# Loads of q and k on ScalarE's queue, and six conversions instead of eight in the first stage behind a rotary attention

## The chip, the cores and the metric

The kernel runs on one core of a Trainium2 chip. The metric is the device time of one execution in microseconds. The engines are TensorE (PE, matmuls), VectorE (DVE), ScalarE (ACT), GpSimd (POOL) and SyncE (SP), which only issues DMA transfers. Each works through its own instructions in the order in which the program has them; they wait for each other with semaphores, and the transfers that they issue run beside them.

## The reference

```python
q_rot, k_rot = (rotate(q), rotate(k))              # q, k, v: (4, 8, 576, 64), rotary positions
scores = scale * np.matmul(q_rot, k_rot.transpose(0, 1, 3, 2))
attn = softmax(scores)                              # over the last axis
x = np.matmul(attn, v)                              # then (2304 tokens, 512)
...
h = x @ w_in                                        # 512 -> 2048
g = np.where(h >= 1, h, np.where(h <= -1, 0.0, (h + 1) ** 2 / 4))
x = g @ w_out                                       # 2048 -> 512
...
h = x @ w_in2
r = np.maximum(h, 0.0)
out = (s * (r * r) + b) @ w_out2
```

## The kernel before

**Numbers.** Every product is made of three matmuls on two halves (hi and lo) of each operand, so all operands are split: hi by a copy on ACT, lo by a subtraction on POOL or DVE. The weights of the two MLPs arrive as 64-bit words and are *converted* to such halves, 512 columns at a time (`Slice.convert`, L126): ACT L133, DVE L134 to L137, ACT L138, and four pieces on POOL (L96). A conversion needs a raw tile (`wraw`, two buffers, load at L144) and two scratch tiles (`wa`, `wm`) from one of two pools with one buffer each, chosen by the half of the slice. A weight slice is one sixteenth of the hidden units of a layer, and has two halves. Some halves are converted early and *parked* in device memory (`parkd`), from where they are later only loaded (`w<-parkd`, L153).

**Attention.** The heads go in 16 pairs, each with 9 units of 128 rows, so 144 units. For a unit: scores on PE (`sc`, L352, two buffers), row maxima on DVE (`nm`, L354), exponentials on ACT (`p`, L359), transposes and the product with v on PE. For pair i, while pair i-1 is being computed, `rope_pair` rotates q and k (POOL and DVE); `lay_q` writes q's halves to `qs` (ACT L306, DVE L307, the last readers of the q tile), and `lay_k` leaves k's halves in the loaded tile, from where SP copies them to `kh` (L323, four transfers) and `kz` (L324, two). The tiles of q and k are loaded by `load_qk` (L261, 576 KB each) two pairs ahead, for pair i+2 at units 4 (q) and 6 (k) of pair i (`do_load`). There are four buffers (`QB`), so q of pair i+2 takes the memory of q of pair i and has to wait until `qs` of pair i is written; k of pair i+2 waits until the copies `kh<-kin` and `kz<-kin` of pair i have landed. From unit 48 on, work of the first MLP on finished tokens is run between the units (`beside`, results added up in device memory as `yd`, tiles `ys` and `yq`, L498 to L506); conversions and parking also lie there.

**Stages.** Behind the attention `stage` (L694) does the rest of the first MLP in three calls: a (the last tokens, 3 chunks of 288, with the first half of the hidden units, `set_a`), b (4 chunks, the second half, `set_b`) and c (2 more). A stage is a loop over chunks and slices; step (c, f) makes the hidden units f of chunk c (`hps`, then ACT L201 and L202, DVE L204, ACT `gh` L102, DVE `gl` L106), and the second layer (`yps`, L764 to L766) follows three steps (`GL`) later. The slices that the next stage needs stand in the list `pending`, one entry for each half. At each step that counts (not step 0 of the first chunk and not the first three of a later one) `owed` grows by `per`, and for each whole one `convert_next` converts the next entry; parked entries at the head of the list are loaded at once by `load_next`.

**Order.** The order of the instructions on PE behind the attention is that of the code; on the other engines, and within the attention, a scheduler sets it when the kernel is built, from priorities and from `issue_after` marks, and it lays each DMA on the queue of the engine that the code names.

Of the kernel before, what the change touches and what calls it, by code (L numbers as in the profile page):

```python
# [66 lines left out]
def kernel(ctx, tc, qq, kk, vv, tab, ww1, ww2, s, b, out):  # L67
    nc = tc.nc
    dram = ctx.enter_context(tc.tile_pool(name="dram", bufs=1, space=DRAM))
    xd = dram.tile([KD, P, NT], F32, name="xd")  # L70
    xp = dram.tile([2, KD, P, NT], F32, name="xp")
    yd = dram.tile([GA // G1, KD, P, NT], F32, name="yd")
    zd = dram.tile([KD, P, NT], F32, name="zd")
    y1d = dram.tile([KD, P, NT], F32, name="y1d")
# [150 lines left out]
    set_a = [Slice(wpa, ww1, f, ROOMS[f]) for f in range(GA)]  # L225
    scratch = [wst]
    set_b = [Slice(None, ww1, f, ROOMS[f - GA], parkd) for f in range(GA, NF)]
# [29 lines left out]
    def load_qk(i, nm, pieces=WHOLE):  # L257
        bb, hp = divmod(i, NP)
        t = att2.tile([P, 2, S], F32, tag="qkin", name=f"{nm}in", bufs=QB)
        for c in pieces:  # L260
            nc.sync.dma_start(out=t[:, :, c], in_=(qq if nm == "q" else kk)[bb, hp, :, :, c])  # L261
        qk_in[nm, i] = t

    def load_v(i):
# [188 lines left out]
    def load_parts(x, n0, n):  # L453

        for t in range(2):
            nc.sync.dma_start(out=x[t].bitcast(F32), in_=parts_at(t, n0, n))
        return x
# [53 lines left out]
    for c in HALVES:  # L511
        nc.sync.dma_start(out=tab_sb[:, :, c], in_=tab[:, :, c])
        if c is HALVES[0]:
            load_qk(0, "k", HALVES)
    load_qk(0, "q", HALVES)
    tq, tk = qk_in.pop(("q", 0)), qk_in.pop(("k", 0))

# [14 lines left out]
    with tc.issue_after(first):  # L532
        load_qk(1, "k")
        load_qk(1, "q")
        load_v(0)
        nc.sync.dma_start(out=s_sb, in_=s.to_broadcast([P, 1]))
        nc.sync.dma_start(out=b_sb, in_=b.to_broadcast([P, 1]))
# [115 lines left out]
    set_c = [Slice(wpa, ww2, f, ROOMS[f]) for f in range(GA)]  # L653
# [40 lines left out]
    def parts_tiles(n):  # L694
        return [qx.tile([P, KD, n], F32R, tag=t, name=t + "2") for t in ("xh", "xl")]
# [316 lines left out]
    def cut(n0, n1, n):  # L1012

        k = -(-(n1 - n0) // n)
        at = [n0 + (n1 - n0) // 16 * i // k * 16 for i in range(k + 1)]
        return [(a, b - a) for a, b in zip(at, at[1:])]
# [5 lines left out]
    a, b, c, d = cut(last, NT, N2A), cut(0, last, N2), cut(last, NT, N2), cut(0, NT, N2)  # L1022
# [45 lines left out]
    def mix(one, two):  # L1068

        both = []  # L1070
        for i, sl in enumerate(one):
            both += [sl] + two[i * len(two) // len(one):(i + 1) * len(two) // len(one)]
        return both

    twice = lambda sls: [sl for sl in sls for _ in range(2)]
    left = twice(set_d[:4] + set_d[7:])
# [22 lines left out]
    first_b, first_c1 = [], []  # L1099

    def ahead_of(chunk, tiles):
        tiles.extend(parts_tiles(chunk[1]))
        load_parts(tiles, *chunk)

    stage(xd, a, yd[0], None, set_a, act1, twice(set_b), 0.5, after=lambda: ahead_of(b[0], first_b))
    assert not pending
    stage(None, b, y1d, yd[1], set_b, act1, mix(left, twice(set_c)), 0.85, ready=first_b, after=lambda: ahead_of(c[0], first_c1))
    stage(None, c, y1d, yd[0], set_b, act1, [], 0.9, lambda i, mark: front_c(i + GA - 1, mark), ready=first_c1)
    convert_next()
    assert not pending and not raws2 and not stores  # L1110
# [66 lines left out]
```

## Time and profile before

| | us |
|---|---|
| three runs, median (lowest to highest) | 1131.36 (1127.6 to 1132.65) |
| profiled execution, its own time | 1134.72 |
| its span, first to last instruction | 1132.9 |
| busy: PE / DVE / ACT / POOL | 1082.3 / 776.5 / 630.0 / 424.7 |
| mean granted TensorE clock | 0.989 |

In the profiled execution the attention without MLP work between the units runs to about 145 us, with it to about 446, stage a to about 548, stage b to about 668 and stage c to about 720; then the second MLP follows. "SPq" in a row is SP's sequencer issuing a transfer. A row of the waits says which line on which engine waited for which, how long in total, how many times, and the longest.

### The profile page before, as it was taken

Reading aid. Unit: us, or ns where it says so; the run is one execution under the profiler, and the core shown is the slowest. Engines: PE = TensorE matmul, PEld = TensorE weight load, DVE = VectorE, ACT = ScalarE, POOL = GpSimd, SP = SyncE. Lnnn points to the kernel's source line nnn. Section 1 sums busy time; section 2 is a strip of 40 time slices with the busy share of each in tenths; the row PEclk is TensorE's granted clock in tenths of the full one; section 3 lists DMA queues with packets and bytes.
Section 4 is the critical chain, followed back from the end, with each engine's and each line's share of the span. In section 5 each row is a group of like instructions: output and inputs, shape, how many; then the busy total and the mean of one; then the engine's idle time right before and its main releaser. Section 6 shows DMA issues by size and latency. Waiting matters only on the chain.

```text
span 1132.9 us, 20034 instructions
## 1 busy us (share of the span) xinstructions
PE 1082.3 (96%) x7296; PEld 990.5 (87%) x7296; DVE 776.5 (69%) x1449; ACT 630.0 (56%) x1430; POOL 424.7 (37%) x564
## 2 busy tenths in 40 slices
PE   3998898989999999999999999999999999999998
PEld 3666687778988989989999999999999999999997
DVE  6888887776676663365566656975877767667754
ACT  4777776765667765455454545475445438334421
POOL 7869886975453241343344444500211110000000
PEclk9999898999999999999999999999999999999999
DMA  7565855665667652854567662521242753221210
GB/s 224 164 174 170 236 154 177 206 174 177 197 190 216 175 173 85 269 171 130 179 203 239 211 230 89 161 68 46 73 143 90 263 172 107 81 64 59 80 61 35
DMA packets 109762, 173.24 MB, mean 153 GB/s; under 512 B 29408, under 2 KB 80608, under 8 KB 109664
## 3 DMA queue, kind: packets, MB, share of 16 engines
q1 hardware_dynamic: 109664, 171.97, 48.5%
q8 instruction: 57, 0.93, 0.4%
q14 instruction: 41, 0.34, 0.1%
HBM read 110.10 MB, written 48.56 MB: 140 GB/s over the span
## 4 chain that ended last, share of the span: by engine, by line
PE 71%; DVE 8%; DMA 8%; POOL 5%; issue 3%; ACT 3%; SPq 1%; POOLq 0%; DVEq 0%; ACTq 0%
PE sum L914 13%; PE hps L180 12%; PE yps L830 6%; PE yps L828 6%; PE yps L829 6%; PE sc L352 5%; PE h L180 3%; PE av L400 3%; PE tp L374 3%; PE y L180 3%; PE yps L765 3%; PE yps L766 3%; PE yps L764 3%; DMA yd<-yq 2%; POOL kin L96 2%
## 5 line engine op out<-in xcount | busy, mean ns | idle before, releaser
L180 PE MATMUL hps<-xh,w 128*128 128x288 f32 (+4 forms) x640 | 164.0, 325 | 0.0
L354 DVE TENSOR_REDUCE nm<-sc 128x1 f32<-128x576 f32 x144 | 107.9, 751 | 43.5 <-PE sc L352 42.6
L352 PE MATMUL sc<-kh,qs 128*128 128x288 f32 x336 | 105.5, 335 | 28.4 <-ACT p L359 16.7
L359 ACT ACTIVATE p<-sc,nm 128x576 f32<-128x576 f32 x144 | 106.7, 744 | 33.5 <-DVE nm L354 32.7
L922 ACT ACTIVATE four<-four,b_sb,s_sb 128x480 f32<-128x480 f32 x64 | 47.3, 782 | 138.1 <-DVE four L921 138.1
L830 PE MATMUL yps<-gh,w 128*128 128x480 f32 (+1 forms) x320 | 118.6, 370 | 0.0
L828 PE MATMUL yps<-gh,w 128*128 128x480 f32 (+1 forms) x320 | 118.4, 370 | 0.0
L829 PE MATMUL yps<-gl,w 128*128 128x480 f32 (+1 forms) x320 | 118.4, 370 | 0.0
L180 PEld LDWEIGHTS hps<-xh,w 128*128 128x128 f32 x640 | 113.7, 189 | 1.0
L96 POOL TENSOR_TENSOR wm<-wm,w 128x256 f32<-128x256 f32 x80 | 70.6, 903 | 105.2 <-ACT w L138 63.6
L352 PEld LDWEIGHTS sc<-kh,qs 128*128 128x128 f32 x336 | 65.8, 198 | 47.7 <-ACT p L359 25.8
L180 PE MATMUL hps<-xl,w 128*128 128x288 f32 (+4 forms) x320 | 103.8, 324 | 0.0
L352 PE MATMUL sc<-kz,qs 128*128 128x288 f32 x336 | 96.5, 306 | 0.0
L764 PE MATMUL yps<-gh,w 128*128 128x288 f32 (+3 forms) x288 | 93.5, 325 | 2.5 <-ACT gh L102 1.9
L374 PE MATMUL tp<-ident,p 128*128 128x128 f32 x576 | 90.8, 283 | 5.1 <-ACT p L359 3.3
L765 PE MATMUL yps<-gl,w 128*128 128x288 f32 (+3 forms) x288 | 93.6, 325 | 0.7 <-DVE gl L106 0.7
L766 PE MATMUL yps<-gh,w 128*128 128x288 f32 (+3 forms) x288 | 93.4, 324 | 0.0
L374 PEld LDWEIGHTS tp<-ident,p 128*128 128x128 f32 x576 | 73.1, 145 | 8.1 <-ACT p L359 3.7
L180 PE MATMUL y<-gh,w 128*128 128x288 f32 x320 | 74.8, 305 | 3.5 <-ACT pt L377 1.7
L180 PE MATMUL h<-xh,w 128*128 128x288 f32 x320 | 74.0, 308 | 2.9 <-DVE gl L106 2.9
L400 PE MATMUL av<-pt,vin 128*64 128x256 f32 (+1 forms) x512 | 76.1, 422 | 0.2
L106 DVE TENSOR_TENSOR gl<-hps,gh 128x288 fp32r<-128x288 f32 (+4 forms) x88 | 46.2, 526 | 34.1 <-ACT gh L102 34.1
(154 smaller groups left out, 2846.1 us busy)
## 6 DMA issues: line engine op xcount, KB each, us to landing
wraw<-in_ww SPq DMA_DIRECT2D x58, 512.0 KB, 4.5
w<-parkd SPq DMA_DIRECT2D x24, 512.0 KB, 6.6
parkd<-wraw SPq DMA_DIRECT2D x18, 512.0 KB, 3.0
kin<-in_k SPq DMA_DIRECT2D x15, 576.0 KB, 5.0
qin<-in_q SPq DMA_DIRECT2D x15, 576.0 KB, 4.2
kh<-kin SPq DMA_DIRECT2D x60, 144.0 KB, 2.6
xs<-y1d SPq DMA_DIRECT2D x32, 240.0 KB, 2.6
xd<-u SPq DMA_DIRECT2D x16, 288.0 KB, 2.5
```

The source lines that it names most:

```text
L180: m = nc.tensor.matmul(out_ps, l, r, start=(i == 0), stop=(i == n - 1))
L352: nc.tensor.matmul(sc[:, half, o:o + n], l, r[:, k0:k0 + n], start=m == 0, stop=m == len(todo) - 1)
L354: maxs[i * 9 + k] = nc.vector.tensor_reduce(out=nm, in_=sc[:, :, :288], axis=AX.XY, op=ALU.max, negate=True).ins
L374: m = nc.tensor.transpose(v[:, c, :], p[:, c * P:(c + 1) * P], ident)
L400: nc.tensor.matmul(ps[j * D:(j + 1) * D, :n], v[:, kt, j, :], pt[g][:, kt, j, :], start=kt == 0, stop=False)
L764: nc.tensor.matmul(acc, wh, gh, start=f == 0, stop=False)
L765: nc.tensor.matmul(acc, wh, gl, start=False, stop=False)
L766: nc.tensor.matmul(acc, wl, gh, start=False, stop=last)
L828: nc.tensor.matmul(acc, wh, gh, start=f == 0, stop=False)
L829: nc.tensor.matmul(acc, wh, gl, start=False, stop=False)
L830: nc.tensor.matmul(acc, wl, gh, start=False, stop=last)
L914: nc.tensor.matmul(acc, l, r, start=j == 0, stop=j == len(t) - 1)
```

## The change

Two things. In `load_qk` the loads of q and k for pairs 2 to 15 (14 + 14 transfers) are issued by ACT instead of SP. And the first stage converts or loads ahead for six slices of `set_b` instead of all eight (12 entries, of which 6 are parked, instead of 16 with 8 parked), at 0.36 for each counting step instead of 0.5, so 6 conversions instead of 8; the second stage begins with the two slices left over (two loads of parked halves, two conversions) and has 0.88 for each step instead of 0.85, which is 19 conversions instead of 18, and the third stage does 9 instead of 8. The total is unchanged.

```diff
@@ load_qk
-            nc.sync.dma_start(out=t[:, :, c], in_=(qq if nm == "q" else kk)[bb, hp, :, :, c])
+            (nc.scalar if i > 1 else nc.sync).dma_start(out=t[:, :, c], in_=(qq if nm == "q" else kk)[bb, hp, :, :, c])
@@ the calls of stage
-    stage(xd, a, yd[0], None, set_a, act1, twice(set_b), 0.5, after=lambda: ahead_of(b[0], first_b))
+    stage(xd, a, yd[0], None, set_a, act1, twice(set_b[:6]), 0.36, after=lambda: ahead_of(b[0], first_b))
     assert not pending
-    stage(None, b, y1d, yd[1], set_b, act1, mix(left, twice(set_c)), 0.85, ready=first_b, after=lambda: ahead_of(c[0], first_c1))
+    stage(None, b, y1d, yd[1], set_b, act1, twice(set_b[6:]) + mix(left, twice(set_c)), 0.88, ready=first_b, after=lambda: ahead_of(c[0], first_c1))
     stage(None, c, y1d, yd[0], set_b, act1, [], 0.9, lambda i, mark: front_c(i + GA - 1, mark), ready=first_c1)
```

The scheduler then puts the instructions of the attention into another order in places. Where the load of q and k for pair 12 stands shows what moves. On SP before, `kin_2705` is k of pair 10, whose memory `kin_3526` (k of pair 12) takes; `qin_3439` is q of pair 12:

```order
L144 DMA wraw_3248<-in_ww1 128x512
L451 DMA xp_58<-xl_2739 128x4x288
L466 DMA xs_3115<-xd_57 128x288
L324 DMA kz0_109<-kin_2705 64x576
L323 DMA kh_2887<-kin_2705 64x576 x4
L324 DMA kz0_109<-kin_2705 64x576
L261 DMA qin_3439<-in_q 128x1152
L144 DMA wraw_3441<-in_ww1 128x512
L261 DMA kin_3526<-in_k 128x1152
L268 DMA vin_2936<-in_v 128x5x64
```

On ACT now, at the same units (`qs0` is pair 10's, `qin_2642` its q tile, whose memory `qin_3439` takes):

```order
L306 ACTIVATE qs0_107<-qin_2642 64x576
L133 ACTIVATE wa_3044<-wraw_3042 128x512
L359 ACTIVATE p_2763,sums_2438<-sc_2773,nm_2778 128x576
L261 DMA qin_3439<-in_q 128x1152
L414 ACTIVATE sume_2867<-sums_2438,eps_67 128x4
L138 CAST w_2357<-wm_3045 128x512
L433 COPY r_2805<-rm_2800 128x384
L379 COPY pt_2765<-tp_2829 128x4x128
L359 ACTIVATE p_2818,sums_2810<-sc_2811,nm_2816 128x576
L261 DMA kin_3526<-in_k 128x1152
L359 ACTIVATE p_2818,sums_2810<-sc_2835,nm_2840 128x576
```

The two loads have left SP, where raw weights and v now follow the copies of pair 10 directly; on ACT the q load stands behind an exponential, and the k load between two exponentials.

On SP at the start of stage a, before (`yd<-yq` are the last stores of `beside`, `wraw_6264` a raw load for the stage's conversions):

```order
L717 DMA xs2_6458<-xd_57 128x288
L451 DMA xp_58<-xl2_6058 128x4x288
L144 DMA wraw_6264<-in_ww1 128x512
L506 DMA yd_59<-yq_5882 128x288
L506 DMA yd_59<-yq_5901 128x288
L498 DMA yq_5920<-yd_59 128x288
L498 DMA yq_5939<-yd_59 128x288
L153 DMA w_6031<-parkd_62 128x2x512 x2
L506 DMA yd_59<-yq_5920 128x288
L153 DMA w_6560<-parkd_62 128x2x512 x2
L506 DMA yd_59<-yq_5939 128x288
L153 DMA w_6261<-parkd_62 128x2x512 x2
```

And now:

```order
L717 DMA xs2_6443<-xd_57 128x288
L451 DMA xp_58<-xl2_6058 128x4x288
L506 DMA yd_59<-yq_5882 128x288
L506 DMA yd_59<-yq_5901 128x288
L498 DMA yq_5920<-yd_59 128x288
L498 DMA yq_5939<-yd_59 128x288
L153 DMA w_6031<-parkd_62 128x2x512 x2
L506 DMA yd_59<-yq_5920 128x288
L153 DMA w_6659<-parkd_62 128x2x512 x2
L506 DMA yd_59<-yq_5939 128x288
L153 DMA w_6327<-parkd_62 128x2x512 x2
L144 DMA wraw_6330<-in_ww1 128x512
```

The raw load has gone from ahead of the stores to behind them and the parked weights; the parked loads still stand among the stores.

On DVE in stage a before, from the eighth block of hidden units (`hps_6281`) on; L134 to L137 with `wa_6267` are one conversion, those with `wa_6478` the next:

```order
L204 SCALAR_TENSOR_TENSOR hps_6281<-hps_6281,ac_6294 128x288
L134 TENSOR_SCALAR wm_6268<-wa_6267 128x512
L106 TENSOR_TENSOR gl_6299<-hps_6281,gh_6298 128x288
L135 SCALAR_TENSOR_TENSOR wm_6268<-wa_6267,wm_6268 128x512
L136 TENSOR_SCALAR wa_6267<-wm_6268 128x512
L134 TENSOR_SCALAR wm_6479<-wa_6478 128x512
L204 SCALAR_TENSOR_TENSOR hps_6314<-hps_6314,ac_6327 128x288
L137 SCALAR_TENSOR_TENSOR wa_6267<-wraw_6264,wa_6267 128x512
L135 SCALAR_TENSOR_TENSOR wm_6479<-wa_6478,wm_6479 128x512
L106 TENSOR_TENSOR gl_6332<-hps_6314,gh_6331 128x288
L136 TENSOR_SCALAR wa_6478<-wm_6479 128x512
L137 SCALAR_TENSOR_TENSOR wa_6478<-wraw_6279,wa_6478 128x512
```

And now, from just ahead of the same block:

```order
L134 TENSOR_SCALAR wm_6250<-wa_6249 128x512
L135 SCALAR_TENSOR_TENSOR wm_6250<-wa_6249,wm_6250 128x512
L136 TENSOR_SCALAR wa_6249<-wm_6250 128x512
L137 SCALAR_TENSOR_TENSOR wa_6249<-wraw_6144,wa_6249 128x512
L204 SCALAR_TENSOR_TENSOR hps_6261<-hps_6261,ac_6274 128x288
L106 TENSOR_TENSOR gl_6279<-hps_6261,gh_6278 128x288
L204 SCALAR_TENSOR_TENSOR hps_6294<-hps_6294,ac_6307 128x288
L134 TENSOR_SCALAR wm_6502<-wa_6501 128x512
L106 TENSOR_TENSOR gl_6312<-hps_6294,gh_6311 128x288
L135 SCALAR_TENSOR_TENSOR wm_6502<-wa_6501,wm_6502 128x512
L136 TENSOR_SCALAR wa_6501<-wm_6502 128x512
L137 SCALAR_TENSOR_TENSOR wa_6501<-wraw_6330,wa_6501 128x512
```

The conversions follow one another where two had been interleaved, with three instructions of the stage between them.

## Rows read from the trace of the kernel before

**Rows 1.** By stretch: busy PE, PEld, DVE, ACT, POOL; PE's clock, DMA share, GB/s.

```profile
25.00:145.00 120.00, 110.02 (x768) 80.21 (x767) 100.04 (x167) 86.45 (x202) 100.40 (x133) 0.97 0.66 188
145.00:446.00 301.00, 284.59 (x2169) 251.22 (x2169) 209.58 (x377) 201.27 (x494) 164.19 (x226) 0.98 0.58 173
446.00:550.00 104.00, 100.83 (x736) 99.79 (x731) 48.43 (x99) 53.78 (x132) 39.26 (x48) 0.98 0.63 203
550.00:668.00 118.00, 118.00 (x721) 118.00 (x720) 74.64 (x142) 59.69 (x123) 52.01 (x68) 1.00 0.57 192
```

**Rows 2.** PE's waits, 28 to 145 us: total, times, longest.

```profile
PE sc L352 <- ACT p L359: 9.4, 11, 1.8
```

**Rows 3.** PE's waits, 145 to 445 us.

```profile
PE sc L352 <- ACT p L359: 5.0, 6, 2.1
PE tr L387 <- DVE pt L381: 3.4, 1, 3.4
```

**Rows 4.** PE's waits, 445 to 550 us.

```profile
PE yps L764 <- ACT gh L102: 1.9, 1, 1.9
```

**Rows 5.** Busy time in slices of 10 us of stage a.

```profile
466.00:476.00 10.00, 9.46 (x71) 9.22 (x70) 1.52 (x4) 3.43 (x8) 4.16 (x7) 1.00 0.66 214
...
486.00:496.00 10.00, 8.12 (x60) 7.66 (x58) 8.04 (x14) 5.82 (x14) 9.01 (x11) 1.00 0.61 192
496.00:506.00 10.00, 9.25 (x58) 9.28 (x59) 4.18 (x11) 5.01 (x13) 3.21 (x5) 0.83 0.79 265
```

**Rows 6.** Timeline of DVE from 480 us: start, duration, instruction.

```profile
491.07 0.42 DVE L134 TENSOR_SCALAR wm<-wa 128x512 uint32<-128x512 uint32 x1
...
494.77 1.10 DVE L137 SCALAR_TENSOR_TENSOR wa<-wraw,wa 128x512 f32<-128x512 uint16 x1
495.80 0.45 DVE L204 SCALAR_TENSOR_TENSOR hps<-hps,ac 128x288 f32<-128x288 f32 x1
```

**Rows 7.** The chain of waits, 460 to 500 us: start, duration, piece.

```profile
474.94 6.76 DMA yd<-yq
```

**Rows 8.** Timeline of SP from 462 us.

```profile
464.29 0.33 SPq L144 DMA_DIRECT2D wraw<-in_ww  x1
464.93 1.59 SPq L506 DMA_DIRECT2D yd<-yq  x2
```

**Rows 9.** Line L261, 28 to 445 us: ns min/median/max; waiters; landing.

```profile
L261 SPq DMA_DIRECT2D qin<-in_q x13: 333/529/584, 30.3 to 324.4; - x13
...
  POOL qin L96: 22.0, 10
...
DMA to landing us min/median/max: 3.8/5.0/8.4
```

**Rows 10.** SP's waits, 28 to 445 us.

```profile
SPq L261 <- DMA kz<-kin: 10.1, 11, 2.5
...
SPq L261 <- DVE qs L307: 3.6, 3, 1.7
...
SPq L261 <- DMA kh<-kin: 3.6, 3, 2.7
```

**Rows 11.** Timeline of SP from 222 us.

```profile
228.30 0.54 SPq L324 DMA_DIRECT2D kz<-kin  x1
229.43 0.34 SPq L261 DMA_DIRECT2D qin<-in_q  x1
...
234.21 0.33 SPq L261 DMA_DIRECT2D kin<-in_k  x1
```

**Rows 12.** Timeline of ACT from 224 us.

```profile
229.96 0.74 ACT L359 ACTIVATE p<-sc,nm 128x576 f32<-128x576 f32 x1 [0.44 <-DVE nm L354]
...
231.44 0.74 ACT L359 ACTIVATE p<-sc,nm 128x576 f32<-128x576 f32 x1 [0.66 <-DVE nm L354]
```

**Rows 13.** Timeline of DVE from 224 us.

```profile
226.06 0.75 DVE L307 SCALAR_TENSOR_TENSOR qs<-qin,qs 64x576 fp32r<-64x576 f32 x1
```

**Rows 14.** The chain of waits, 160 to 200 us.

```profile
166.94 6.02 DMA qin<-in_q
```

**Rows 15.** Busy time and granted clock in a slice of 5 us.

```profile
190.00:195.00 5.00, 4.55 (x19) 4.54 (x20) 4.16 (x8) 4.16 (x11) 2.00 (x3) 0.50 0.36 115
```

## The prediction

> **What bounds the kernel now.** I read the busy time of each engine by stretch first, then TensorE's (PE's) waits in each stretch, then the two places where those waits end: the queues of SyncE (SP) and ScalarE (ACT). In the sixteen pairs of the attention, 25 to 446 us, PE is busy 110.02 of 120 us and then 284.59 of 301 us; in stage a it misses 3.2 us of 104, and in stage b nothing [rows 1]. So only 10.0 + 16.4 + 3.2 us of idle time are to be had, and what a lowered clock costs behind the gaps. In the unfilled part (one pair's work alone) PE waits almost only for the exponentials on ACT: 9.4 us in 11 waits [rows 2]. VectorE (DVE), busy 100.04 of 120 us, is the engine that sets the pace there, and ACT with 86.45 has 28% free [rows 1]. In the filled part (pairs and MLP work interleaved) the exponentials account for 5.0 us in 6 waits, one single wait for `pt` for 3.4 [rows 3]. In stage a the longest wait is one of 1.9 us for `gh` [rows 4]; the slices of 10 us show where: 0.54 us missing at 466 to 476, 1.88 at 486 to 496, 0.75 at 496 to 506, and in the last of these the granted clock is 0.83, between the two levels of 1.2 and 2.4 GHz, after the gap [rows 5].
>
> **The stop in stage a.** Read backwards it goes as follows. PE waits for `gh`, which waits for DVE's L204 at 495.80; ahead of that on DVE lie two conversions interleaved, among them the L134 at 491.07 and the L137 at 494.77 [rows 6]. They are bunched because the conversion before them began late: ACT's L133 waited for a store `yd<-yq` that took 6.76 us to land from 474.94 [rows 7], since the scratch of this conversion lies on the memory of that tile. The store was issued behind parked weights, and its forerunner at 464.93 behind a raw weight load of 512 KB at 464.29 [rows 8].
>
> **The change, stage a.** Eight conversions become six, on every third step instead of every second; none is left among the first six blocks of hidden units, the raw load ahead of `yd<-yq` is gone, and the two interleaved conversions become two in sequence (the order rows above). What is to be had is the idle time 0.54 + 1.88 + 0.75 = 3.2 us and the clock, 10 us at 0.83, so 1.7 us: 4.9 in all [rows 5]. The other end is 0: the wait of ACT for the last `yd<-yq` is still there, three conversions still follow one another behind it, and DVE still carries the whole second one ahead of the next L204. I take −4, near the full size, because one conversion fewer lies in the bunch, and four DVE instructions of up to 1.10 us [rows 6] are more than the 1.9 us that PE waited.
>
> **The change, stage b.** Two conversions and two loads of parked weights go there. Two conversions are eight DVE instructions, at 1.10 us each 8.8 us at most; DVE has 118 − 74.64 = 43 us free in that stretch, while PE is never idle [rows 1]. I cost them at nothing. The cover is gone if the last slice, converted in the third and fourth step and read in the eighth, came late; then PE would stand as in stage a, for about 1.9 us [rows 4]. Stage c ends with one conversion more to do in a stretch where PE waits for nothing: nothing as well.
>
> **The change, the issue of the loads.** 28 loads leave SP's queue and enter ACT's. One issue took 333 to 584 ns on SP [rows 9]. All on the path would be 28 × 0.53 = 14.8 us; all in ACT's free time, 0. An issue costs PE time if it lies in a unit where PE already waits for an exponential; that was so in 11 + 6 of the 144 units [rows 2, 3]. 28 × 17/144 × 0.43 gives +1.4 us, which I take.
>
> **What ACT now waits for.** A load waits for its buffer, and on ACT everything behind it waits too. SP stood at L261 for 10.1 us for `kz<-kin`, 3.6 us for `qs` and 3.6 us for `kh<-kin` [rows 10]; nothing urgent stood behind it. On ACT the exponentials do. The clearest place is the k load of pair 12: SP issued it at 234.21, when the copies out of the buffer (the last issued at 228.30) had landed [rows 11]. ACT now has it between two exponentials, of which the first ran from 229.96 and the second from 231.44 [rows 12]. If the copies land as before, ACT stands until 234.2, some 2.8 us past the time at which it began the second exponential. At the other loads the same two views show no place with as long a hold. So this term lies between 0 (copies land sooner, PE has a second score buffer in hand) and four such holds, 11.2 us. I take one, +2.8.
>
> **What SP's queue gains.** The q load of pair 12 was free to go when DVE's L307 ended at 226.8 [rows 13] and was issued at 229.43 [rows 11], 2.6 us late, because SP stood at copies for pair 10; it then took some 5 us [rows 9] to land. POOL waited 22.0 us for q loads, ten times [rows 9]. If 2.6 of 2.6 + 5.0 us is the queue's part, POOL's waits shrink by a third, 7.5 us. All of it at PE would be −7.5; none if POOL's lead hides it. I take half less a little, −3.5: that POOL's lateness reaches PE at times is shown by the wait for `pt` [rows 3], which the chain of waits follows back to the landing of a q load [rows 14], though that one, by the end of its L307, was issued without delay.
>
> The rows show, then, that lateness in the queue and not the issue alone is what SP adds. The Trainium skill ("DMA: Bandwidth & Descriptors", section "Issuing engines are not separate DMA queues") says that transfers started by the scalar, sync or gpsimd engine run on the same 16 DMA engines and interleave, and that more issuing engines save only the time to start them, usually small. By that rule the last term is near 0 and the sum 1131.6; by the rows it is −3.5.
>
> **The sum.** −4 + 0 + 1.4 + 2.8 − 3.5 = −3.3 us. The profiled execution took 1134.72 us, with a span of 1132.9; the terms are all parts of its span. The median of the three runs is 1131.36, 0.3% lower, and the terms carry over to it unchanged: 1131.36 − 3.3 = 1128.
>
> **Rivals.** (B) The attention gains in earnest: q loads land sooner everywhere, −7.5, ACT is never held, stage a gives its full −4.9, and one fall of the clock such as the 0.50 at 190 to 195 us (2.5 us) [rows 15] goes with its gap: 1131.36 − 7.5 − 4.9 − 2.5 + 1.4 = 1118. For it: ACT's free time, POOL's 22.0 us [rows 9]. Against: the pace of the unfilled part is DVE's. (C) Slower: ACT is held at the head of its queue by loads whose copies have not landed. Four holds of 2.8 us, and the clock's fall of 2.5 us behind the longest gap [rows 15]: 1131.36 + 11.2 + 2.5 + 1.4 − 3.5 − 4 = 1139. It decides from the third hold on. For it: the place at pair 12 and the 10.1 us [rows 10, 11, 12]; against: in most other places the release comes before ACT gets there. (D) Stage a keeps its stop, because ACT still waits for `yd<-yq` and the conversions still bunch: 1131.36 + 1.4 + 2.8 − 3.5 = 1132. (E) The loads land no sooner, because what they wait for (the buffer, then the shared DMA engines) is what it was; ACT pays, and only stage a gains: 1131.36 − 4 + 1.4 + 2.8 = 1131.6. This is what the rule quoted above would have.
>
> **How the numbers follow.** Forecast 0.36 (1123 to 1133), B 0.30, C 0.15, D 0.11, E 0.08. About 0.5%, 5.7 us, is what a measurement of this kernel can tell from no change, so faster means under 1125.7 and slower over 1137.0. Faster: nearly all of B and a quarter of the forecast, 0.40. Slower: most of C and the tails of D and E, 0.16. Same: 0.44. The range goes from 1114 (beyond B's 1118, as its terms may each be some larger) to 1140 (just past C's 1139); it leaves out about half of C and a fifth of B.
>
> **What would show it.** Stage a: no PE idle time of over 1 us between 480 and 510 us, the granted clock at 1.00 there, and the time from the stage's start to its end about 4 us shorter; if the 1.9 us wait for `gh` is still there, D holds. Attention: POOL's waits for q loads down from 22.0 to about 15 us, if they stay at 22 E holds; ACT waits at L261 of 3 to 5 us in all, with one of 2 to 3 us near the k load of pair 12; if ACT's holds come to over 8 us and PE's waits for exponentials grow from 14.4 us by as much, C holds; if PE's idle time between 25 and 446 us falls from 26.4 to under 20 us, B. The prediction is wrong as a whole if the stages behind 550 us, where PE is never idle, move by more than 1 us.

## The result: slower by 1.1%, and the profile after

The changed kernel takes 1142.46 us in the median (1140.49 to 1146.24, 4 runs) against 1129.48 us (1126.8 to 1132.65, 4 runs): a ratio of 1.0109, 95% interval 1.0089 to 1.0128. The forecast was 1128, the range ended at 1140. The profiled execution took 1142.62 us, with a span of 1140.5, 7.6 us more than that of before; that one lay some 4 us above its kernel's median, so the two traces show about three fifths of the loss.

Where it comes from is read from four marks, the start of the same instruction in both traces (us):

| first matmul of the second layer | before | after | shift |
|---|---|---|---|
| in stage a | 468.1 | 474.6 | +6.5 |
| in stage b | 550.7 | 552.6 | +1.9 |
| in stage c | 678.3 | 680.8 | +2.5 |
| behind stage c | 752.9 | 760.3 | +7.4 |

So in these two executions the attention loses 6.5 us, stage a gives 4.6 back, and stages b and c lose 5.5, which I had costed at nothing. From there on nothing moves. (Stage c's last matmul stands at 744 us in the trace of before, not at about 720 as said above.) How much of each shift is chance is read below, from more executions.

The stretches of after, with the columns of [rows 1]:

```profile
25.00:145.00 120.00, 108.62 (x774) 79.30 (x772) 101.76 (x168) 86.25 (x202) 99.81 (x133) 0.98 0.67 187
145.00:446.00 301.00, 278.51 (x2112) 244.90 (x2111) 206.31 (x374) 198.05 (x491) 164.94 (x226) 0.97 0.57 172
446.00:550.00 104.00, 103.46 (x774) 102.09 (x774) 45.62 (x93) 51.62 (x128) 33.66 (x40) 1.00 0.59 191
550.00:668.00 118.00, 117.72 (x718) 117.43 (x717) 75.69 (x142) 60.42 (x125) 52.13 (x65) 1.00 0.56 181
```

PE is idle for 33.9 us of the 421 us to 446, 7.5 more than before. Its waits in 145 to 455 us, against the 5.0 us of [rows 3]:

```profile
PE sc L352 <- ACT p L359: 14.8, 10, 5.2
PE tr L387 <- DVE pt L381: 2.7, 1, 2.7
```

The exponentials came late. ACT's timeline at the place that the prediction names, the loads of pair 12:

```profile
227.20 0.36 ACTq L261 DMA_DIRECT2D qin<-in_q  x1
...
230.24 0.74 ACT L359 ACTIVATE p<-sc,nm 128x576 f32<-128x576 f32 x1 [0.37 <-DVE nm L354]
230.88 0.19 ACT L359 ACTIVATION_READ_ACCUMULATOR p<-sc,nm 128x1 f32 x1
237.86 0.34 ACTq L261 DMA_DIRECT2D kin<-in_k  x1
238.24 0.74 ACT L359 ACTIVATE p<-sc,nm 128x576 f32<-128x576 f32 x1 [7.17 <-DMA kz<-kin]
```

The first exponential begins as in [rows 12], 229.96 there; the second begins at 238.24 where it had begun at 231.44. Between the two ACT stood 7 us at the k load, because the copies out of its buffer had not landed. PE's granted clock fell behind it, as in [rows 15]; the slices of 5 us:

```profile
235.00:240.00 5.00, 0.87 (x3) 0.87 (x4) 0.00 (x0) 1.76 (x4) 2.69 (x4) 0.82 0.62 166
240.00:245.00 5.00, 5.00 (x24) 3.10 (x25) 4.81 (x8) 3.27 (x9) 3.69 (x5) 0.50 0.15 60
```

What this hold costs is read from the exponentials. From the one behind which ACT now has the q load to the fourth after it 8.7 us pass before, and 15.7 us after:

```profile
226.54 0.75 ACT L359 ACTIVATE p<-sc,nm 128x576 f32<-128x576 f32 x1
...
235.22 0.73 ACT L359 ACTIVATE p<-sc,nm 128x576 f32<-128x576 f32 x1
```

```profile
226.35 0.72 ACT L359 ACTIVATE p<-sc,nm 128x576 f32<-128x576 f32 x1
...
242.07 0.74 ACT L359 ACTIVATE p<-sc,nm 128x576 f32<-128x576 f32 x1
```

In the traces of five runs below whose attention is that of before it is 8.7 to 9.2 us. It was not the only place at which ACT stood. From the end of what ACT did before a load to the load's issue, summed over the 14 q loads, ACT stood for 2.2 us; over the 14 k loads 28.0 us, ten of them with over 1.3 us each.

### The profile page after: what moved, and what is told of

Its sections match the earlier page's. It is cut to its first block, busy times and chain, and to the rows that moved or that the text cites. A ratio compares the mean times of both kernels' runs of the same rounds, so it can differ in the third digit from the quotient of the medians.

```text
span 1140.5 us, 20036 instructions
## 1 busy us (share of the span) xinstructions
PE 1080.0 (95%) x7296; PEld 986.4 (86%) x7296; DVE 777.7 (68%) x1449; ACT 626.5 (55%) x1430; POOL 427.5 (37%) x564
## 5 line engine op out<-in xcount | busy, mean ns | idle before, releaser
L134 DVE TENSOR_SCALAR wm<-wa 128x512 uint32<-128x512 uint32 x64 | 30.3, 473 | 70.6 <-ACT wa L133 69.9
```

## The experiments

All times are medians of rounds in which the kernel before was run on the same chip (medians 1129.67 to 1130.73); the ratio is to that.

**Each part alone.** First only the loads:

```diff
-            nc.sync.dma_start(out=t[:, :, c], in_=...
+            (nc.scalar if i > 1 else nc.sync).dma_start(out=t[:, :, c], in_=...
```

> Only the loads of q and k from pair 2 on are issued by ACT; the stages are those of the kernel before. Theory 1: the loss lies in the attention, where ACT stands at the head of its queue for k loads whose buffers are not yet copied out (10.9 us in 3 waits in the changed kernel, the longest 7.2). Then the attention ends 6 to 7 us later than before, the stop in stage a (1.9 us for gh, clock 0.83) is back, stage c loses nothing, and the time is 6 to 8 us over before, about 1136 to 1138. Theory 2: the loss is in the later stages and the attention's part is chance: within 2 us of before.

1142.12 us, ratio 1.0100 (1.0079 to 1.0122). The loads alone carry the loss; theory 2 falls. Theory 1 has the place right and the size too small (11.5 us over, not 6 to 8); of the stop in stage a PE's wait for `gh` is back (1.6 us), the lowered clock behind it is not. Then only the stages, as in the diff of the change, with the attention of before:

> Only the stages are changed; all loads of q and k are issued by SP, and the attention is the kernel before's, instruction for instruction. Theory 1: stage a is 4 to 5 us shorter and stage c some 5 us longer, because conversions there wait for raw loads that now are issued behind the stores of stage b: together within 1 us of before, about 1130. Theory 2 (stage c's loss is only what a later attention leaves behind, and does not come with the changed split): 4 to 5 us under before, about 1125.

1132.3 us, ratio 1.0014 (1.0000 to 1.0029). Theory 1, with 1.6 us over by the ratio: stage a's gain and the loss in b and c nearly cancel. Its attention is the one of before, instruction for instruction, and yet ended 5.9 us earlier than in the profile of before: a few us of the attention are chance from one execution to the next.

So is a part of the stop in stage a. In this and every other trace with the new stages, stage a (first mark to second) is 4.6 us shorter than in the profile of before; but in five traces with the old stages (loads alone, q alone, k alone, and two runs with late k loads) it is 2.8 to 3.2 us shorter too. PE's wait for `gh` is there in all five, with 1.2 to 1.6 us instead of the 1.9 of [rows 4], but no fall of the clock follows it; in the traces with the new stages there is no such wait. One of the five (late k, loads on SP), 450 to 545 us:

```profile
PE yps L765 <- ACT gh L102: 1.3, 1, 1.3
```

The new split is worth that wait, 1.4 to 1.8 us, not 4.6.

**The longest hold alone.** The changed kernel with one load put back:

```diff
-            (nc.scalar if i > 1 else nc.sync).dma_start(...
+            (nc.scalar if i > 1 and (nm, i) != ("k", 12) else nc.sync).dma_start(...
```

> The changed kernel with one instruction moved back: the k load of pair 12 is issued by SP again; every other instruction stands where it did on its engine. Theory 1 (one hold of ACT, 7.2 us at this load, makes most of the loss in the attention): ACT goes on with its exponentials, PE loses its wait of 5.2 us at 239 us, and the time falls by 5 to 7 us, to about 1136. Theory 2 (DMA is so crowded there that the copies and loads come late for everyone): SP or POOL waits instead, PE stops a few us later for scores of the next pair, and the time falls by under 2 us, to about 1141.

1142.64 us, ratio 1.0109 (1.0086 to 1.0132): nothing gained, theory 1 in this form is wrong. The edit did work at its place: the four exponentials from there take 10.3 us instead of 15.7. But PE now stops at 251 to 255 us, where in the changed kernel it waited 1.0 us. Its waits in 236 to 264 us:

```profile
PE y L180 <- DVE ptr L392: 2.7, 1, 2.7
PE tr L387 <- DVE gl L106: 1.3, 1, 1.3
```

That is theory 2's sign, though it gives back only about half of the gain; and this profile came to the place 3.5 us later than that of the changed kernel, with the same instructions up to there. Why the medians show no gain at all is not settled. ACT still stands at the other k loads, here 3.6 us each at those of pairs 6 and 11:

```profile
87.13 0.33 ACTq L261 DMA_DIRECT2D kin<-in_k  x1
87.51 0.74 ACT L359 ACTIVATE p<-sc,nm 128x576 f32<-128x576 f32 x1 [3.95 <-DVE pt L381]
...
205.49 0.33 ACTq L261 DMA_DIRECT2D kin<-in_k  x1
205.87 0.58 ACT L379 COPY pt<-tp 128x512 f32<-128x512 f32 x1 [3.94 <-DMA kz<-kin]
```

(The bracket names the event that came last by the profile. What the load of pair 6 waits for are pair 4's copies: the last was issued at 81.57 and took 5.5 us to land.) The 13 k loads left on ACT held it for 18.7 us. The longest piece of a loss that is spread over ten places need not be the loss.

**q or k alone.** With the stages of before:

```diff
+            (nc.scalar if i > 1 and nm == "q" else nc.sync).dma_start(...    # q alone
+            (nc.scalar if i > 1 and nm == "k" else nc.sync).dma_start(...    # k alone
```

> The stages of before; only the q loads from pair 2 on are issued by ACT, k loads stay on SP. Theory 1 (k loads hold ACT, q loads do not, since their buffer is freed by DVE just before): ACT's waits at L261 come to under 3 us, the attention ends within 2 us of before, and the time is within 2 us of before, or some 2 us under it if POOL's waits of 22.0 us for q loads shrink. Theory 2 (the 28 issues and the new order on ACT are what costs): half of the loss in the attention, 3 to 4 us over before.

1131.92 us, ratio 1.0013 (0.9999 to 1.0028): theory 1, though ACT stood 3.5 us and not under 3.

> The stages of before; only the k loads from pair 2 on are issued by ACT, q loads stay on SP. Theory 1 (k loads hold ACT): ACT stands 20 us or more at L261, and the time is 8 to 11 us over before, about 1140. Theory 2 (both together make the loss, by the order they bring): half of it or less, 1133 to 1136.

1131.64 us, ratio 1.0002 (0.9987 to 1.0017). Theory 1 falls, and theory 2 asked for some loss, where none is seen: neither load alone costs what both cost. ACT stood 10.0 us here, at most 1.7 at once, at the same units, to within two, at which it stands 21.9 us with both. What differs is when the copies land that the k load waits for. The landing times of `kz<-kin` (L324), 28 to 345 us, in order: before, k alone, q alone, loads alone, the changed kernel:

```profile
DMA to landing us min/median/max: 2.3/2.7/6.9
```

```profile
DMA to landing us min/median/max: 2.3/2.6/4.2
```

```profile
DMA to landing us min/median/max: 2.3/4.2/7.9
```

```profile
DMA to landing us min/median/max: 2.3/4.0/8.3
```

```profile
DMA to landing us min/median/max: 2.3/4.4/9.8
```

In the other runs it is the same with one exception: the median is 2.8 to 3.0 us in five with the q loads on SP, 3.6 to 4.1 in three with them on ACT, but 3.0 in the last run, which has them on ACT too. On SP the q load stands behind the last copy of its pair; on ACT it can go out before it, and does so at eight of 13 pairs in the changed kernel, against one before. At 56.57 us, for instance, it went out between the copies of its pair: the three issued ahead of it landed in 2.5 to 3.0 us, the three behind it in 5.2 to 5.4. The same place (pair 11) on SP before, and on SP and ACT after:

```profile
198.77 0.54 SPq L324 DMA_DIRECT2D kz<-kin  x1
199.41 0.54 SPq L261 DMA_DIRECT2D qin<-in_q  x1
...
201.50 0.33 SPq L261 DMA_DIRECT2D kin<-in_k  x1
```

```profile
196.71 0.53 SPq L324 DMA_DIRECT2D kz<-kin  x1
198.02 0.34 SPq L144 DMA_DIRECT2D wraw<-in_ww  x1
```

```profile
196.83 0.36 ACTq L261 DMA_DIRECT2D qin<-in_q  x1
...
201.64 0.33 ACTq L261 DMA_DIRECT2D kin<-in_k  x1
```

On ACT the q load of 576 KB starts together with the copy of 144 KB, which then took 4.8 us to land instead of 2.6; the raw weights (512 KB) follow the copy at the same distance as before. The k load comes 4.4 us behind the end of the last copy's issue instead of 2.2, with ACT standing at it. With q alone that lateness is there too, but it is SP that stands: its waits at L261, which in [rows 10] were 10.1 and 3.6 us, are in that kernel

```profile
SPq L261 <- DMA kz<-kin: 21.4, 12, 4.9
SPq L261 <- DMA kh<-kin: 10.9, 8, 3.3
```

and the time shows nothing urgent behind them on SP. The account that fits these four kernels is that the loss takes both: q on another queue makes the copies late, and k on ACT turns their lateness into late exponentials.

**The wait taken away.** On the kernel with both loads on ACT, the k load is placed later, when the copies have landed:

```diff
-                    load_qk(i + 2, "q" if k == 4 else "k")
+                    with tc.issue_after(exps[n - 11]) if k == 6 and n > 11 else ExitStack():
+                        load_qk(i + 2, "q" if k == 4 else "k")
```

> The loads of q and k on ACT as in the changed kernel, the stages of before, but each k load from pair 4 on is held back until 11 units before the unit at which the code asks for it, which puts it 2 to 5 units later on ACT, when its buffer's copies should have landed. Theory 1 (ACT's standing at k loads, 22 to 28 us in the traces of the two kernels that have them there, is the loss): the standing falls under 5 us and the time falls by 8 to 11 us against the kernel with both loads on ACT (1142.1), to 1131 to 1134. Theory 2 (the new order of the attention, or the 28 issues, is the loss, and the standing is idle time of ACT that would be there anyway): within 3 us of 1142. Theory 3 (k comes too late for its rotation): POOL and PE wait for k instead, over 1142.

1127.7 us, ratio 0.9979 (0.9963 to 0.9995). ACT stands 0.5 us at the k loads, though the copies land as late as with both loads (median 4.0 us, at most 7.7). At the k load of pair 12 nothing stands any more:

```profile
238.34 0.74 ACT L359 ACTIVATE p<-sc,nm 128x576 f32<-128x576 f32 x1 [2.99 <-DVE nm L354]
238.50 0.33 ACTq L261 DMA_DIRECT2D kin<-in_k  x1
```

Theory 1, with more than it asked for: 14 us of 1142 are gone with the standing, and the 28 issues, which are all still there, cost nothing that can be seen. The edit is not clean, though. With the k loads the scheduler moved about a quarter of the instructions of ACT and DVE in the attention, while the three slow kernels (loads alone, the changed kernel, and pair 12's load on SP) share nearly one order. That this order costs something by itself is not excluded. PE's waits for exponentials, 28 to 445 us, are 25.2 and 25.3 us in the first two of these, 12.3 to 14.6 in the six traces with the attention of before, and 18.0 here; but with pair 12's load on SP they are 19.1 and in the next run 19.5, and those two are 12 us apart.

POOL's waits for the loads, 28 to 445 us:

```profile
  POOL qin L96: 12.3, 8
  POOL kin L96: 9.5, 7
```

For q they are 12.3 us against 22.0 in [rows 9], but in five more traces with the attention of before they are 13.8 to 23.3, so that this is no clear gain; waits for k, 0.6 us before, are added.

The same on the whole changed kernel:

> The whole changed kernel, with each k load from pair 4 on placed 2 to 5 units later on ACT. Theory 1 (ACT's standing at k loads is the loss of the whole change, and the stages cost 1.6 us by themselves): ACT's standing falls from 28 us to about 5, and the time from 1142.5 to that of the run with late k loads and the stages of before plus 1.6 us, so 1128 to 1131. Theory 2 (the new stages are worse when the attention ends earlier): 1132 or more.

1130.21 us, ratio 0.9997 (0.9980 to 1.0013): the loss of the whole change is gone with ACT's standing (theory 1). Then the mark for later k loads, with all loads on SP:

> The kernel before with all loads on SP, and each k load from pair 4 on placed by the same later mark as in the run on ACT. It tells whether the 3 us that the late k loads on ACT gained against before come from ACT's queue or from the later time. Theory 1 (from the queue: SP's own copies and loads no longer stand behind L261, where it waited 10 + 3.6 + 3.6 us): no gain here, 1129 to 1134. Theory 2 (from the later time: transfers crowd less): the gain is here too, 1126 to 1129.

1129.25 us, ratio 0.9987 (0.9971 to 1.0003). This run does not tell between its theories, because the mark moved nothing: in the trace every engine has the instructions of the kernel before in the same order. It is the kernel before, measured once more, and shows what chance does. Its profile has a span of 1125.8 us against 1132.9, of which 3.9 us are in the attention and 3.1 in stage a; and its ratio lies as far from 1 as 0.9987. The interval of the late loads on ACT overlaps with this one, so that their 0.2% is not told from no gain.

**The loss in stages b and c.** Loads on SP, the new stages, with more conversions in stage b:

```diff
-    ... mix(left, twice(set_c)), 0.88,
+    ... mix(left, twice(set_c)), 0.91,      # and 1.0 in another run
```

> Loads as before, stages as in the changed kernel but 0.91 instead of 0.88 for each step of stage b, so that 20 conversions are made in stage b and 8 in stage c, as many there as before. Theory 1 (the ninth conversion in stage c makes the 5 us lost there): stage c takes what it took before, the 1.7 us gained in stage a stay, and the time is 1 to 2 us under before. Theory 2 (what is lost comes from which conversions fall at the change from stage b to c, those whose raw load stands behind the stores of stage b or whose raw buffer is still to be parked): some loss of 2 to 5 us is left, and the time is 0 to 3 us over before.

1134.02 us, ratio 1.0037 (1.0022 to 1.0052): theory 2, a little beyond its 3 us. Stages b and c lose 6.5 us against the profile of before (5.2 with 0.88), though stage c has no more to do than before: 5.1 of them lie in b now, where it was 1.4 of 5.2.

> As the run with 0.91, with 1.0: 22 conversions in stage b, one at every step that counts, 6 in stage c. Theory 1: stage c is shorter still in its waits, none left, and stage b, where VectorE has over 40 us free of 118, hides the two more: 1 to 3 us under before. Theory 2 (conversions at every step of stage b wait for raw loads, ACT stands at L133 and delays gh): PE waits in stage b, 1 to 4 us over before.

1137.82 us, ratio 1.0057 (1.0036 to 1.0079): theory 2 again, beyond its 4 us; more conversions in stage b lose more, 10.0 us in b and c. What ACT waits for at L133, 545 to 760 us, before and in the run with the new stages alone:

```profile
ACT wa L133 <- DMA wraw<-in_ww: 26.3, 10, 6.8
```

```profile
ACT wa L133 <- DMA wraw<-in_ww: 36.2, 14, 6.9
```

(Five more traces with the old stages have 23.0 to 29.2 us, the others with the mixed list 34.1 to 39.1.) It looks like the pattern of the attention: an instruction that waits for a transfer stands at the head of ACT's queue, and `ac` and `gh` of the stage behind it. In the changed kernel PE's waits there, which were none, are

```profile
PE yps L764 <- DVE yp L771: 1.6, 2, 1.4
PE yps L765 <- DVE gl L106: 1.5, 3, 1.0
PE yps L764 <- ACT gh L102: 1.0, 2, 0.7
```

Then the order of the list, parked slices first:

```diff
-    ... twice(set_b[6:]) + mix(left, twice(set_c)), 0.88,
+    ... twice(set_b[6:]) + left + twice(set_c), 0.88,
```

> Only the stages are changed (loads on SP), and the list of stage b has all slices that are parked after their conversion first and those converted in place last, instead of mixed, so that stage c converts in place only. Theory 1 (a raw buffer that must be parked comes free late, the next raw load is issued late, ACT stands at L133 and PE waits for gh, gl and yp): ACT's waits for raw loads in stage c fall from their 36 us, PE's 3.5 us of waits there go, and the time falls by 3 to 5 us against the run with the mixed list (1132.3), to about 1128. Theory 2 (two raw buffers are too few for a conversion at nearly every step, whichever kind): within 2 us of 1132, the waits are then in stage b.

1132.32 us, ratio 1.0013 (0.9995 to 1.0030). In stage c ACT's waits for raw loads are down to 0.2 us, so it is the parked slices that made those; but PE's waits are in stage b now (545 to 665 us):

```profile
PE yps L764 <- ACT gh L102: 1.2, 1, 1.2
PE yps L765 <- DVE gl L106: 1.1, 2, 0.6
```

The time is the same: theory 2, the waits moved. But ACT's waits for raw loads are 18.9 us here, fewer than the 26.3 of before, and stages b and c still take 4.1 us more than there (1.9 in the run that follows, with the same stages). So these waits do not measure the loss. Where PE waits in this run, DVE and POOL are busy most of the time, with conversions among other work:

```profile
645.00:665.00 20.00, 17.69 (x95) 16.43 (x94) 18.28 (x29) 11.34 (x22) 17.27 (x18) 0.91 0.53 184
```

What makes the loss in b and c stays open between raw loads that come late and conversions that bunch on DVE; a third raw buffer was not tried, and that two are too few is not shown. Last, the parked slices first and the late k loads on the changed kernel:

> The changed kernel with late k loads on ACT and the parked slices first in stage b's list. Theory 1 (both causes are found): faster than the kernel before by 3 us from the loads and 2 to 3 us from the stages, about 1125. Theory 2 (only the first): 1128 to 1131, as with late k loads alone.

1130.8 us, ratio 1.0002 (0.9985 to 1.0018): theory 2. The version with late k loads on ACT and the old stages has the lowest median of all, 0.2% under the kernel before, which the control above does not tell from none.

## Why the prediction was wrong

**The step that failed** is "What ACT now waits for". Its mechanism was right and so was the place; rival C is what happened, with 0.15 instead of the highest chance and a time of 1139 instead of 1142.5. The term was 2.8 us, one hold, with four as its end; ACT stood for 28.0 us, 6.8 of them at pair 12 alone, and the late k loads, which take the standing away, were worth 14 us on the kernel with the loads alone, 12 on the whole. The condition "if the copies land as before" is what did not hold. I read when each buffer is released from the trace of before ("no place with as long a hold"). But in that trace the q load stood behind the copies in one queue. The change itself moved the release: the median landing of `kz<-kin` went from 2.7 to 4.4 us. That the hold is passed on to PE is seen at pair 12; that the whole 12 us are holds, and none of them the order of the attention, is not shown. A release time read from a trace holds only as long as the change leaves alone what sets it.

**The rule of the Trainium skill** ("DMA: Bandwidth & Descriptors", section "Issuing engines are not separate DMA queues") was used in the prediction for half of what it says, that starting transfers from a second engine saves only the time to start them. Its other half is that transfers of all issuing engines interleave on the same 16 DMA engines. The landing of `kz<-kin` agrees, 2.7 us before and 4.4 after: a q load that is let go beside the copies delays them.

**SP's queue** was to gain 3.5 us. POOL's waits for q are 25.5 us in the changed kernel against 22.0, and 13.8 to 23.3 in five more executions of the same attention as before; no gain. With the late k loads they are 12.3 and 16.3. **The issues** were to cost 1.4 us; one took 334 to 364 ns, and the kernels with late k loads, which have all 28 on ACT, show no cost.

**Stage a** came out as forecast in the trace, 4.6 us for 4, and its clock between 496 and 506 us is 1.00. But most of that was the chance of one profile: 2.8 to 3.2 us of it come without the edit. The stop itself belongs to the old stages, with a wait of 1.2 to 1.6 us for `gh`; its full length and the fall of the clock behind it, which the forecast took for a property of the program, were those of one execution.

**Stages b and c** were costed at nothing because PE never waited there and DVE was free. DVE's free time, summed over the stretch, was no cover: in every trace with the new stages PE waits in b or c, for `gh`, `gl` or `yp`. Whether ACT's waits at L133 for raw loads (26.3 us before, 36.2 with the new stages, but 18.9 with the parked slices first) or conversions that bunch on DVE make them stays open. Together the new stages are worth +1.6 us (0 to 3.3), not −4.

**The signs that the prediction named** did their work: ACT's holds over 8 us and PE's waits for exponentials up from 14.4 to 25.3 us say C (before, six executions have 12.3 to 14.6); stages behind 550 us that move by over 1 us say that the whole was wrong.

## What to carry to other kernels

Before a load goes to the queue of an engine that computes, ask what the load waits for, and what stands behind it: a wait that did no harm on SP held every later instruction on ACT. Two moves that are each harmless can lose together, if one delays the event that the other then waits for; time each alone and both. Place such a load where its buffer has long been free, and don't take release times from a trace in which the transfers went out in another order. Compare the two traces' orders before you read an edit as a test: one here moved nothing, and another moved much more than it meant to.

## What the runs showed of the hardware

A copy of 144 KB between two tiles, with the q load behind it in its own queue, landed in 2.6 to 3.0 us in the medians of seven traces (at most 8.0); with that load, of 576 KB, let go from another engine's queue, often before it, it took 3.6 to 4.4 us in the medians of six traces, 3.0 in a seventh (at most 9.8). A load at the head of ACT's queue whose buffer was not free held the exponentials behind it for up to 6.8 us. And two executions of the same program had spans of 1132.9 and 1125.8 us; the same attention ended up to 5.9 us apart, more than the new stages were worth.
